# A later transpose of the softmax sums, and a short token chunk moved from last to third, in a fused attention and MLP kernel

## The chip, the cores and the metric

The kernel runs on one core of a Trainium2 chip. The metric is the device time of one execution in microseconds. Three runs of the kernel before took 754.11, 754.46 and 759.69 us; the median is 754.46 us. The profile comes from another execution, which took 759.01 us.

## The reference

Four batches, eight heads, 576 tokens, head size 64. Attention has a position bias that is itself a small network; its output, with the heads side by side, is a matrix of 2304 tokens by 512, which goes through a two-layer MLP with a squared ReLU.

```python
scores = np.matmul(q, k.transpose(0, 1, 3, 2)) / np.sqrt(D)
x = (np.log1p(np.abs(rel)) / psi_i)[..., None]
bias = np.maximum(x @ w1 + b1, 0.0) @ w2            # 8 heads, 576 x 576
scores = scores + bias.transpose(2, 0, 1)[None]
attn = np.exp(scores - np.max(scores, axis=-1, keepdims=True))
attn = attn / (np.sum(attn, axis=-1, keepdims=True) + 1e-09)
x = np.matmul(attn, v)   # then tokens x 512
h = x @ w_in             # 512 -> 2048
g = s * np.maximum(h, 0.0) ** 2 + b
return g @ w_out         # 2048 -> 512
```

All of it is float32. The kernel gets that from TensorE by splitting an operand into a high and a low part and adding three products (high by high, high by low, low by high).

## The kernel before, in words

There are three stages. In the first, to about 60 us, the bias of all heads is computed and written to DRAM. In the second, attention runs over 16 *pairs*: a pair p is one head of two batches. In the third, the MLP runs over chunks of tokens. The order of instructions on every engine is the program's own, written out by hand; each engine works through its queue in order and waits on semaphores.

A pair has five blocks of rows, numbered t or u from 0 to 4. Blocks 0 to 3 are 128 rows of each of the two batches; block 4 holds the last 64 rows of both in one tile of 128. The attention loop has 80 steps; `step(n)` with n = 5p + u works on three pairs' stages at once:

- the scores of block m = n + 2 (`scores`, line 228): TensorE writes them to PSUM, one tile for each of the two batches (`width`), out of a pool of two tiles;
- `biased` (line 242), on VectorE, adds the bias and takes the row maximum, once for each of these tiles, which it thereby gives back;
- `expo` (line 253), on ScalarE, exponentiates and adds up each row into a column of the pair's tile `su`;
- `probs_t` transposes the exponentials of block n on TensorE, through two PSUM tiles of the pool `ps_t`: part 2 (line 307) is the 128 columns at the seam of the two batches, part 0 and part 1 four transposes each (line 298). In u = 4 there are only part 1 (line 318) and part 0 (line 313), in this order. ScalarE (lines 303, 308, 320) and VectorE (305, 315) copy them to SBUF;
- `av` multiplies the transposed exponentials of the pair before, p - 1, with V (lines 333 and 336). Its last call, in u = 4, scales the result with the reciprocals of the sums (line 341, VectorE) and stores it (line 342, SP's queue);
- `fill` does the next piece of a background job, the decoding of the MLP's weights from their raw words: ScalarE (line 373), GpSimd (375), and three VectorE instructions (377, 380, 383), in a cycle of five; the weights of the first group are also split into parts (392, 395). A step does one or two such pieces, two where u is even. The raw words are loaded (line 360) two tiles ahead.

GpSimd also splits q and k of the next pair (lines 203 and 204), in u = 0 and u = 1.

The sums reach line 341 in this way. In u = 3 all sums of the pair are there, and `norm` (lines 265 and 266, VectorE) takes their reciprocals. `norm_t` transposes the 128 x 9 tile on TensorE into a free part of the PSUM tile of part 2 (line 270), and VectorE copies it out (line 272). `norm_store` writes it to DRAM with four small DMAs (278, 280), `norm_load` (285) reads it back as two broadcast rows in the layout of line 341. These DMAs stand in SP's queue with all other loads and stores.

In the third stage a chunk of n tokens takes 16 steps f. `expand` (line 430) makes 128 hidden features of all n tokens in 12 matmuls, ScalarE and VectorE apply the squared ReLU (434, 435, 439, 440), and `project` (line 454), two steps behind, adds their part to n/128 output tiles in PSUM with three matmuls each. At f = 15 each output tile is copied out (462, 464) and stored (465). The tokens of the next chunk are loaded (411) at f = 10 to 13 and split (419, 420) at f = 12 to 15. 2304 tokens make four chunks of 512 and one of 256, which is the last.

Of the kernel before, what the change touches and what calls it, by code (L numbers as in the profile page):

```python
# [26 lines left out]
def attention_moe(ctx, tc, q, k, v, w_in, w_out, dist, par, out):  # L27
# [3 lines left out]
    NT = out.shape[0]  # L31
# [10 lines left out]
    LAST = 5 * NP  # L42
# [144 lines left out]
    def load_q(p):  # L187
        if p < NP:
            h, b0 = pairs[p]
            qs[p] = io.tile([128, 640], F32, tag="qt", name="qt")  # L190
            nc.sync.dma_start(out=qs[p], in_=q[b0 // 2, h])

    def load_k(p):
        if p < NP:
            h, b0 = pairs[p]
            ks[p] = io.tile([128, S + 64], F32, tag="kt", name="kt")
            nc.sync.dma_start(out=ks[p], in_=k[b0 // 2, h])
# [16 lines left out]
    def scores(n):  # L214
        p, t = divmod(n, 5)
        qt, kt = qs[p], ks[p]
        c = slice(128 * t, 128 * t + 128)
        xs = range(width(n))
        ps = [ps_s.tile([128, 2, 512], F32, tag="s", name="sps") for _ in xs]
        mms = []  # L220
        for hf in range(2):
            for x in xs:
                d = slice(64 * x, 64 * x + 64) if t < 4 else slice(0, 128)
                o = hf * HALF + (64 if x == 0 else 0)
                for i, (a, b) in enumerate(((0, 0), (0, 1), (1, 0))):
                    mms.append((i, hf, x, ps[x][:, hf, 0:HALF], qt[d, a, c], kt[d, b, o:o + HALF]))
        for i, _, _, o, a, b in sorted(mms, key=lambda e: e[1::-1]):
            nc.tensor.matmul(o, a, b, start=(i == 0), stop=(i == 2))  # L228
        units[n] = (
            tp.tile([128, 2, S], F32, tag="pr", name="pr"),  # L230
            sm.tile([128, 2], F32, tag="mn", name="mn"),
            ps,
        )
        if t == 0:
            sums[p] = sm.tile([128, 9], F32, tag="su", name="su")

    def biased(n, x):
        p, t = divmod(n, 5)
        _, mn, ps = units[n]
        bias = bts[group[p]][:, t, 64 - 64 * x:64 - 64 * x + S] if t < 4 else bes[p]  # L240
        tt = tp.tile([128, S], F32, tag="tt", name="tt")
        nc.vector.tensor_tensor_reduce(  # L242
            tt.rearrange("p (a b) -> p a b", a=2), ps[x][:, :, 0:HALF],
            bias.rearrange("p (a b) -> p a b", a=2),
            -1.0 / ROOT, BIG, ALU.add, ALU.min, mn[:, x:x + 1],
        )
        tts[n, x] = tt

    def expo(n, x):
        p, t = divmod(n, 5)  # L250
        pr, mn, _ = units[n]
        col = 4 * x + t if t < 4 else 8
        nc.scalar.activation(  # L253
            pr[:, x], tts.pop((n, x)), AF.Exp, bias=mn[:, x:x + 1], scale=-1.0,
            accum_out=sums[p][:, col:col + 1])

    def width(n):
        return 2 if n % 5 < 4 else 1
# [4 lines left out]
    def norm(p):  # L263
        su = sums.pop(p)
        nc.vector.tensor_scalar(su, su, 1e-9, None, op0=ALU.add)
        nc.vector.reciprocal(su, su)
        rows[p] = su

    def norm_t(p, ps):
        nc.tensor.transpose(ps[0:9, 128:256], rows.pop(p), ident)  # L270
        rt = sm.tile([9, 128], F32, tag="rt", name="rt", bufs=2)
        nc.vector.tensor_copy(rt, ps[0:9, 128:256])
        rts[p] = rt

    def norm_store(p):
        rt = rts.pop(p)
        for x in range(2):
            nc.sync.dma_start(
                out=rs_d[p][x, 0:512].rearrange("(t j) -> t j", j=128), in_=rt[4 * x:4 * x + 4, :])
            nc.sync.dma_start(out=rs_d[p][x:x + 1, 512:S], in_=rt[8:9, 64 * x:64 * x + 64])  # L280

    def norm_load(p):
        rbs[p] = tp.tile([128, S], F32, tag="rb", name="rb", bufs=2)
        for x in range(2):
            nc.sync.dma_start(out=rbs[p][64 * x:64 * x + 64, :], in_=rs_d[p][x:x + 1, :].broadcast_to([D, S]))

    def probs_t(n, part):
        p, t = divmod(n, 5)
        pr = units[n][0]
        if p not in pts:  # L290
            pts[p] = (ptp.tile([128, 4, 2, S], F32, tag="pt", name="pt"),
                      ptp.tile([128, S], F32, tag="ptr", name="ptr"))
        pt, ptr = pts[p]
        ps = ps_t.tile([128, 512], F32, tag="t", name="tps")
        c = slice(128 * t, 128 * t + 128)
        if t < 4 and part < 2:
            for kb in range(4):
                nc.tensor.transpose(  # L298
                    ps[:, 128 * kb:128 * kb + 128],
                    pr[:, part, 64 * part + 128 * kb:64 * part + 128 * kb + 128], ident)  # L300
            o, i = pt[:, :, part, c], ps.rearrange("p (a b) -> p a b", a=4)
            if part == 0:
                nc.scalar.activation(o, i, AF.Copy)  # L303
            else:
                nc.vector.tensor_copy(o, i)  # L305
        elif t < 4:
            nc.tensor.transpose(ps[:, 0:128], pr.rearrange("p x j -> p (x j)")[:, 512:640], ident)  # L307
            nc.scalar.activation(ptr[:, c], ps[:, 0:128], AF.Copy)  # L308
            if t == 3:
                norm_t(p, ps)  # L310
        elif part == 0:
            for kb in range(4):
                nc.tensor.transpose(  # L313
                    ps[:, 128 * kb:128 * kb + 128], pr[:, 0, 128 * kb:128 * kb + 128], ident)
            nc.vector.tensor_copy(
                pt[:, :, :, 512:S], ps.rearrange("p (a x b) -> p a x b", a=4, x=2))
        else:
            nc.tensor.transpose(ps[0:64, 0:128], pr[:, 0, 512:S], ident)  # L318
            for x in range(2):
                nc.scalar.activation(  # L320
                    ptr[64 * x:64 * x + 64, 512:S], ps[0:64, 64 * x:64 * x + 64], AF.Copy)

    def av(p, kb, hf):
        h, b0 = pairs[p]
        pt, ptr = pts[p]
        vt = vals[p]
        if kb == 0 and hf == 0:
            accs[p] = ps_x.tile([128, 2, 512], F32, tag="x", name="xps")
        ps = accs[p]
        c = slice(hf * HALF, (hf + 1) * HALF)  # L330
        if kb < 4:
            for x in range(2):
                nc.tensor.matmul(ps[64 * x:64 * x + 64, hf, 0:HALF], vt[:, 4 * x + kb, :], pt[:, kb, x, c],  # L333
                                 start=(kb == 0), stop=False)
        else:
            nc.tensor.matmul(ps[:, hf, 0:HALF], vt[:, 8:10].rearrange("p i d -> p (i d)"), ptr[:, c],  # L336
                             start=False, stop=True)
        if kb == 4 and hf == 1:
            xs = rbs.pop(p)
            xv = xs.rearrange("p (a b) -> p a b", a=2)  # L340
            nc.vector.tensor_tensor(xv, ps[:, :, 0:HALF], xv, op=ALU.mult)
            nc.sync.dma_start(out=xt_d[b0 // 2][:, h * D:(h + 1) * D, :], in_=xs)
# [52 lines left out]
        nc.gpsimd.tensor_tensor(lo, full, hi.bitcast(F32), op=ALU.subtract)  # L395


    chunks = [(t0, min(512, NT - t0)) for t0 in range(0, NT, 512)]
    NC = len(chunks)
    xs_t, gs_t, os_t = {}, {}, {}  # L400

# [66 lines left out]
    def ok(n, x):  # L468
        return 0 <= n < LAST and x < width(n)
# [7 lines left out]
    def step(n):  # L477
        p, u = divmod(n, 5)
        m = n + 2
        cur = 0 <= n < LAST  # L480
        if ok(m, 0):
            scores(m)
            biased(m, 0)
        if cur and u == 3:
            norm(p)
        if ok(m, 1):
            biased(m, 1)
        if cur:
            for part in (2, 0, 1) if u < 4 else (1, 0):
                probs_t(n, part)  # L490
        if ok(m, 0):
            expo(m, 0)
        if ok(m, 1):
            expo(m, 1)
        if p >= 1:
            av(p - 1, u, 0)
            av(p - 1, u, 1)
            fill()
            if u % 2 == 0:
                fill()  # L500
        if 0 <= n < LAST:
            if u == 3:
                load_be(p + 1)
                load_q(p + 3)
                load_k(p + 3)
                norm_store(p)
            if u == 4:
                norm_load(p)
            if u < 2:
                split_qk(p + 1, u)  # L510
            if u == 4:
                load_v(p + 2)
            for e in loads_at.get((p, u), ()):
                load_bias(*e)
# [14 lines left out]
    def fill():  # L529
        next(filler, None)  # L530
# [189 lines left out]
```

## Time and profile before

| | |
|---|---|
| median of three runs | 754.46 us |
| the profiled execution | 759.01 us, its span 757.0 us |
| TensorE busy (matmuls) | 722.6 us, 95% of the span |
| VectorE busy | 428.3 us, 57% |
| ScalarE busy | 362.5 us, 48% |
| GpSimd busy | 185.4 us, 24% |
| mean granted TensorE clock | 0.991 |
| longest entries of the chain that ended last | line 430 26%, line 454 26%, line 228 8%, line 333 7%, line 298 7% |

Busy shares are means over the whole span, in which the three stages have different limits. Matmuls are pipelined and the ends of their bars are modelled, so starts are surer than ends. PE is TensorE's matmuls, PEld its weight loads, DVE VectorE, ACT ScalarE, POOL GpSimd and SP the engine from whose queue the DMAs are issued (SPq).

### The profile page before, as it was taken

How to read it: one execution, taken by the hardware profiler on the slowest of the kernel's cores; microseconds unless marked ns; L12 is line 12 of the kernel's file. 1: busy time of each engine (PE TensorE's matmuls, PEld its weight loads, DVE VectorE, ACT ScalarE, POOL GpSimd, SP SyncE). 2: the span in 40 equal slices, each digit the busy share in tenths (PEclk: the TensorE clock that was granted, in tenths of full speed). 3: DMA queues.
4: the chain of work that ended last, by engine and by line, in shares of the span. 5: the costliest groups of instructions: out<-in, count | busy, mean ns of one | idle time of the engine just before them, and what ended most of it. 6: DMA issues, size and time to landing. Idle time of an engine off the chain costs nothing.

```text
span 757.0 us, 12033 instructions
## 1 busy us (share of the span) xinstructions
PE 722.6 (95%) x4530; PEld 538.3 (71%) x4530; DVE 428.3 (57%) x794; ACT 362.5 (48%) x756; POOL 185.4 (24%) x194
## 2 busy tenths in 40 slices
PE   8978989898999999999999999999999999999998
PEld 5436666565666666666888888888888888888896
DVE  7966867687787877894369742233323333232332
ACT  7967656465666666664454432223222232222332
POOL 7990524344141252310755200000000000000000
PEclk9999999899999999999999999999999999999999
DMA  5878654545363664334012121000300002000100
GB/s 168 281 219 265 196 181 156 181 156 209 128 209 128 211 225 156 128 114 172 17 38 88 42 79 34 1 1 0 112 1 0 1 1 83 1 1 0 57 1 28
DMA packets 39817, 76.98 MB, mean 102 GB/s; under 512 B 9040, under 2 KB 12368, under 8 KB 39760
## 3 DMA queue, kind: packets, MB, share of 16 engines
q1 hardware_dynamic: 39616, 75.90, 30.7%
q8 instruction: 35, 0.57, 0.3%
q10 hardware_dynamic: 144, 0.33, 0.1%
q14 instruction: 22, 0.18, 0.1%
HBM read 55.45 MB, written 20.13 MB: 100 GB/s over the span
## 4 chain that ended last, share of the span: by engine, by line
PE 81%; POOL 6%; DVE 5%; issue 4%; DMA 2%; SPq 1%; ACT 1%; POOLq 0%; DVEq 0%
PE hps L430 26%; PE o L454 26%; PE sps L228 8%; PE xps L333 7%; PE tps L298 7%; POOL f L119 4%; DVE tt L242 3%; PE xps L336 2%; PE tps L307 1%; PE tps L313 1%; DMA raw<-in_moe_w_in_dram 1%; PE tps L318 0%; SPq L154 0%; DMA pt__110<-in_par_dram 0%; POOL kr L204 0%
## 5 line engine op out<-in xcount | busy, mean ns | idle before, releaser
L454 PE MATMUL o<-who,gt 128*128 128x512 f32 x576 | 192.4, 393 | 0.0
L430 PE MATMUL hps<-x,whi 128*128 128x512 f32 (+1 forms) x640 | 183.7, 371 | 0.0
L435 DVE SCALAR_TENSOR_TENSOR r<-r,sb 128x512 f32<-128x512 f32 (+1 forms) x80 | 56.7, 709 | 192.3 <-ACT r L434 192.3
L434 ACT ACTIVATE r<-hps 128x512 f32<-128x512 f32 (+1 forms) x80 | 44.5, 557 | 223.7 <-PE hps L430 223.7
L430 PEld LDWEIGHTS hps<-x,whi 128*128 128x128 f32 x640 | 116.9, 188 | 23.8 <-issue 0.4
L454 PEld LDWEIGHTS o<-who,gt 128*128 128x128 f32 x576 | 108.2, 188 | 24.2
L430 PE MATMUL hps<-x,wli 128*128 128x512 f32 (+1 forms) x320 | 118.7, 371 | 0.0
L253 ACT ACTIVATE pr<-tt,mn 128x576 f32<-128x576 f32 x144 | 110.2, 767 | 13.9 <-DVE mn L242 13.4
L242 DVE CUSTOM_DVE_ANT_0 tt<-sps,bt 128x576 f32<-128x576 f32 x128 | 92.3, 749 | 39.6 <-PE sps L228 34.8
L454 PE MATMUL o<-wlo,gt 128*128 128x512 f32 x288 | 113.2, 393 | 0.0
L228 PEld LDWEIGHTS sps<-kr,qr 64*128 64x128 f32 (+1 forms) x864 | 69.5, 187 | 42.1 <-DVE mn L242 16.9
L228 PE MATMUL sps<-kr,qr 64*128 64x288 f32 (+1 forms) x864 | 90.9, 313 | 6.5 <-POOL kr L204 2.9
L440 DVE SCALAR_TENSOR_TENSOR gt<-r,sb,gt 128x512 fp32r<-128x512 f32 (+1 forms) x80 | 56.3, 704 | 54.0 <-ACT gt L439 54.0
L298 PE MATMUL tps<-ident,pr 128*128 128x128 f32 x512 | 79.6, 285 | 0.9 <-ACT ptr L308 0.3
L439 ACT ACTIVATE gt<-r,sb 128x512 fp32r<-128x512 f32 (+1 forms) x80 | 54.4, 680 | 52.3 <-DVE r L435 52.3
L333 PE MATMUL xps<-pt,vt 128*64 128x288 f32 x512 | 78.4, 430 | 0.0
L298 PEld LDWEIGHTS tps<-ident,pr 128*128 128x128 f32 x512 | 58.5, 144 | 13.4 <-ACT ptr L308 9.0
L430 PEld LDWEIGHTS hps<-x,wli 128*128 128x128 f32 x320 | 60.1, 188 | 11.0
L454 PEld LDWEIGHTS o<-wlo,gt 128*128 128x128 f32 x288 | 54.1, 188 | 11.6
L305 DVE COPY pt<-tps 128x512 f32<-128x512 f32 x64 | 44.0, 688 | 17.4 <-PE tps L298 17.4
L303 ACT ACTIVATE pt<-tps 128x512 f32<-128x512 f32 x64 | 38.3, 598 | 32.0 <-PE tps L298 30.3
L375 POOL TENSOR_SCALAR full<-full 128x512 f32<-128x512 f32 x32 | 21.0, 657 | 127.0 <-ACT full L373 120.6
(69 smaller groups left out, 742.1 us busy)
## 6 DMA issues: line engine op xcount, KB each, us to landing
bias<-stg SPq DMA_DIRECT2D x36, 288.0 KB
raw<-in_moe_w_in_dram SPq DMA_DIRECT2D x16, 512.0 KB
raw<-in_moe_w_out_dram SPq DMA_DIRECT2D x16, 512.0 KB
bt<-bias SPq DMA_DIRECT2D x7, 1152.0 KB
qt<-in_q_dram SPq DMA_DIRECT2D x16, 320.0 KB
kt<-in_k_dram SPq DMA_DIRECT2D x16, 320.0 KB
vt<-in_v_dram SPq DMA_DIRECT2D x16, 320.0 KB
rb<-rs SPq DMA_DIRECT2D x32, 144.0 KB
```

Of the source, the lines that this page charges most:

```text
L228: nc.tensor.matmul(o, a, b, start=(i == 0), stop=(i == 2))
L242: nc.vector.tensor_tensor_reduce(tt.rearrange("p (a b) -> p a b", a=2), ps[x][:, :, 0:HALF], bias.rearrange("p (a b) -> p a b", a=2), -1.0 ...
L253: nc.scalar.activation(pr[:, x], tts.pop((n, x)), AF.Exp, bias=mn[:, x:x + 1], scale=-1.0, accum_out=sums[p][:, col:col + 1])
L298: nc.tensor.transpose(ps[:, 128 * kb:128 * kb + 128], pr[:, part, 64 * part + 128 * kb:64 * part + 128 * kb + 128], ident)
L305: nc.vector.tensor_copy(o, i)
L333: nc.tensor.matmul(ps[64 * x:64 * x + 64, hf, 0:HALF], vt[:, 4 * x + kb, :], pt[:, kb, x, c], start=(kb == 0), stop=False)
L430: nc.tensor.matmul(ps[:, 0:n], w[0, g][:, a, fc], xs_t[c, a][:, j, 0:n], start=(i == 0), stop=(i == 3 * KB - 1))
L434: nc.scalar.activation(r, ps[:, 0:n], AF.Relu)
L435: nc.vector.scalar_tensor_tensor(r, r, sb[:, 0:1], r, op0=ALU.mult, op1=ALU.mult)
L439: nc.scalar.activation(hi, r, AF.Identity, bias=sb[:, 1:2])
L440: nc.vector.scalar_tensor_tensor(lo, r, sb[:, 1:2], hi.bitcast(F32), op0=ALU.add, op1=ALU.subtract)
L454: nc.tensor.matmul(os_t[c][i], gt[:, a, tok], w[1, g][:, fo], start=(f == 0 and j == 0), stop=(f == NF - 1 and j == 2))
```

## The change

There are two parts. In the first, `norm_t` is called one step later, in u = 4 behind part 1 of `probs_t`, and in that PSUM tile; in u = 3, `norm` comes behind both calls of `biased` and no longer between them. The stores of the sums move from u = 3 to u = 4, and the loads from u = 4 to u = 0 of the next pair (for the last pair, to the step n = LAST). In the second part, the chunk of 256 tokens is put third: tokens 1024 to 1280; the chunks behind it start at 1280 and 1792.

```diff
@@ probs_t
         elif t < 4:
             nc.tensor.transpose(ps[:, 0:128], pr.rearrange("p x j -> p (x j)")[:, 512:640], ident)
             nc.scalar.activation(ptr[:, c], ps[:, 0:128], AF.Copy)
-            if t == 3:
-                norm_t(p, ps)
         elif part == 0:
...
             for x in range(2):
                 nc.scalar.activation(
                     ptr[64 * x:64 * x + 64, 512:S], ps[0:64, 64 * x:64 * x + 64], AF.Copy)
+            norm_t(p, ps)
@@ chunks
-    chunks = [(t0, min(512, NT - t0)) for t0 in range(0, NT, 512)]
+    sizes = [512] * (NT // 512)
+    if NT % 512:
+        sizes.insert(len(sizes) // 2, NT % 512)
+    chunks = [(sum(sizes[:i]), n) for i, n in enumerate(sizes)]
@@ step
             biased(m, 0)
+        if ok(m, 1):
+            biased(m, 1)
         if cur and u == 3:
             norm(p)
-        if ok(m, 1):
-            biased(m, 1)
...
+        if n == LAST:
+            norm_load(p - 1)
         if 0 <= n < LAST:
             if u == 3:
                 load_be(p + 1)
                 load_q(p + 3)
                 load_k(p + 3)
+            if u == 4:
                 norm_store(p)
-            if u == 4:
-                norm_load(p)
+            if u == 0 and p > 0:
+                norm_load(p - 1)
```

## Rows read from the trace of the kernel before

**Rows 1.** Busy time by stage: us, each engine's busy us (instructions), PEclk, DMA share, GB/s

```profile
60.00:345.00 285.00, 262.01 (x2028) 177.04 (x2026) 221.02 (x500) 184.01 (x464) 91.74 (x88) 0.98 0.53 175
362.00:702.00 340.00, 340.00 (x1477) 276.99 (x1476) 132.80 (x169) 106.56 (x174) 36.91 (x30) 1.00 0.09 28
702.00:757.00 55.00, 51.28 (x314) 45.43 (x312) 18.43 (x37) 16.11 (x36) 0.00 (x0) 1.00 0.08 29
```

**Rows 2.** Waits, 60 to 345 us: who waited for whom; us in total, times, longest

```profile
PE tps L270 <- DVE su L266: 16.9, 15, 1.2
PEld tps L298 <- DVE rt L272: 3.8, 14, 0.3
PE sps L228 <- POOL kr L204: 2.9, 4, 1.3
```

**Rows 3.** Timeline: start, us, instruction; the scores issued in u=3, u=4, u=0, u=1

```profile
236.18 1.06 PE L228 MATMUL sps<-kr,qr 64*128 64x288 f32 x12
...
241.10 1.07 PE L228 MATMUL sps<-kr,qr 64*128 64x288 f32 x12
...
243.73 1.07 PE L228 MATMUL sps<-kr,qr 64*128 64x288 f32 x12
...
247.17 1.06 PE L228 MATMUL sps<-kr,qr 64*128 64x288 f32 x12
```

**Rows 4.** Timeline inside that u=3; in brackets the idle time before

```profile
237.17 0.33 PE L307 MATMUL tps<-ident,pr 128*128 128x128 f32 x1
...
238.05 0.17 DVE L265 TENSOR_SCALAR su<-su 128x9 f32<-128x9 f32 x1
...
238.62 0.27 PE L270 MATMUL tps<-ident,su 128*9 128x128 f32 x1 [1.12 <-DVE su L266]
...
238.72 1.32 PE L298 MATMUL tps<-ident,pr 128*128 128x128 f32 x8
...
239.06 0.27 DVE L272 COPY rt<-tps 9x128 f32<-9x128 f32 x1
...
239.38 0.42 PEld L298 LDWEIGHTS tps<-ident,pr 128*128 128x128 f32 x4 [0.30 <-DVE rt L272]
...
240.08 0.69 DVE L305 COPY pt<-tps 128x512 f32<-128x512 f32 x1 [0.75 <-PE tps L298]
```

**Rows 5.** Busy time by stretch, one where the clock fell (columns as in rows 1)

```profile
105.50:108.90 3.40, 3.35 (x15) 2.47 (x17) 1.97 (x5) 2.09 (x5) 0.00 (x0) 0.50 0.17 60
```

**Rows 6.** Timeline of VectorE at the end of u=4 and the start of u=0

```profile
243.56 0.69 DVE L315 COPY pt<-tps 128x512 f32<-128x512 f32 x1
...
244.16 0.75 DVE L341 TENSOR_TENSOR rb<-xps,rb 128x576 f32<-128x576 f32 x1
...
244.94 0.76 DVE L242 CUSTOM_DVE_ANT_0 tt<-sps,bt 128x576 f32<-128x576 f32 x1
```

**Rows 7.** Timeline: a decode beside GpSimd's split, and the same decode alone

```profile
179.47 1.54 POOL L204 TENSOR_TENSOR kr<-kt,kr 128x640 fp32r<-128x640 f32 x1
...
179.65 1.91 DVE L380 SCALAR_TENSOR_TENSOR full<-raw,full 128x512 uint32<-128x512 uint32 x1
...
227.40 0.69 DVE L380 SCALAR_TENSOR_TENSOR full<-raw,full 128x512 uint32<-128x512 uint32 x1
```

**Rows 8.** Timeline at the end of attention: stores, load and use of the last sums

```profile
346.56 0.21 SPq L280 DMA_DIRECT2D rs<-rt  x1
...
352.05 1.11 SPq L285 DMA_DIRECT2D rb<-rs  x2
...
360.11 0.74 DVE L341 TENSOR_TENSOR rb<-xps,rb 128x576 f32<-128x576 f32 x1
```

**Rows 9.** Chain that ended last, in the short chunk: start, us, what

```profile
702.37 1.42 PE hps L430 x12
...
715.05 1.41 PE o L454 x6
```

**Rows 10.** Timeline of SP's queue: the four output stores of a long chunk

```profile
625.43 2.22 SPq L465 DMA_DIRECT2D out_dram<-ob  x4
```

## The prediction

> **What bounds the kernel now.** I read the busy time by stage first [rows 1]. From 362 to 702 us TensorE (PE) is busy 340.00 of 340.00 us: five chunks of tokens run there with no gap, over three chunk borders too. So an edit in that stage can win nothing unless it takes matmuls away. The attention stage, 60 to 345 us, is different: PE is busy 262 of 285 us, so 23 us are lost there, while VectorE (DVE) has 64 us of idle time and ScalarE (ACT) 101. No engine is full; the order of waits sets the time.
>
> The second view is the list of waits in that stage [rows 2]. One entry holds most of PE's idle time: 16.9 us in 15 waits, at the transpose of the sums (line 270), for the reciprocal on DVE (line 266). A sibling stands beside it: 3.8 us in 14 waits in which the next transposes wait for the copy of that transpose (line 272), since it holds one of the two PSUM buffers. Waits for GpSimd's split of k are a sixth of the first, 2.9 us.
>
> The third view is the timeline of one pair, read by the start of each step's scores [rows 3]. Step u=3 takes 4.92 us (236.18 to 241.10), u=4 2.63, and u=0 3.44. Step u=3 has the same matmuls as u=0 plus one small transpose, yet lasts 1.48 us longer. Inside it [rows 4] the reason is plain: PE ends the transpose of the small block at 237.5, then DVE must finish the first reduction and both small operations of the norm, the first of which starts at 238.05, and PE starts again at 238.62, 1.12 us idle. Everything after it in the step, the copies and the products with V, is shifted by this.
>
> **The change, part by part.** The profiled execution took 759.01 us, its span 757.0; the three runs have a median of 754.46. The sum is made on the profiled execution and taken off the median.
>
> 1. *The two waits go.* In the new order the norm is computed in u=3 behind both reductions, and its transpose is asked for in u=4, one whole step (some 3.4 us) after. PE then has nothing to wait for: the reciprocal, only some 0.7 us later than now, is ready well before u=4 starts. That removes 16.9 + 3.8 = 20.7 us of waits [rows 2]. The one pair checks it: 1.12 + 0.30 [rows 4] of the 1.48 us by which its u=3 is too long [rows 3]. What is late next in u=3: the scores of u=4 need both PSUM tiles of scores back, which is the end of the second reduction. That reduction moves forward to 238.05, where the norm's first instruction stands now, and lasts 0.76 as the one of rows 6, so it ends near 238.8, while PE, by the pace of u=0, wants it at 236.18 + 3.44 = 239.6. It holds by 0.8 us.
>
> 2. *Clock.* Three of the long u=3 steps are followed by stretches at half the granted clock (1.2 in place of 2.4 GHz), as 105.5 to 108.9 [rows 5]; there are three such stretches, one of them twice as long, and around each PE had stalled twice, for GpSimd's k and for the norm. One of the two stalls goes. What half the clock costs is at most half of 4 x 3.4 us, 6.8, and less by the time in which PE waits; the least is 0. I take 2, since the stall for k stays [rows 2].
>
> 3. *The transpose itself moves to u=4.* It is one of the small transposes, of which eight take 1.32 us [rows 4], or 0.15 to 0.17 each, in a step where PE has no gap (2.63 us). 16 times 0.15 is 2.4 us lost; in u=3 it is given back within the wait already counted.
>
> 4. *The copy of it, 0.27 us* [rows 4], moves on DVE into u=4. There it stands before the copy of probabilities, the scaling of the output and then the first reduction of the next pair, which follow each other at 243.56, 244.16 and 244.94 with no gap [rows 6]. Its cover is that in u=0 PE needs 3.44 us [rows 3] where the loop scores, two reductions, scores needs only 2.63, so a late DVE has 0.8 us to spare. With two decode operations on DVE in that step (0.69 each [rows 7]) the cover is gone and the full 0.27 comes through. Bounds: 0 and 15 x 0.27 = 4.1. Two of five positions of the decode sequence put two such operations there, 6 of 15 pairs: 1.6 us.
>
> 5. *DVE's slack in u=3 goes.* Before, DVE idles in that step while the chain waits, 0.75 us ahead of the copy alone [rows 4]. Afterwards it has two reductions (0.76 each), the norm (0.17 and about as much again), the copy (0.69) and a decode (0.69): 3.2 us of a step of 3.4. The nearest row for a bad case is a decode that ran beside GpSimd's split of k: 1.91 us in place of 0.69 [rows 7]. Such an excess, 1.22 us, is now hidden in part by u=3's slack. Bounds 0 and 15 x 1.22 = 18.3; DVE is idle for 64 us of the stage [rows 1], the copies still have slack in u=1 and u=2, so I take a value near the low end, 1.5 us.
>
> 6. *The DMAs.* The four stores of the sums go to u=4, behind the store of the output on SP's queue, and the two loads to u=0 of the next pair; they are needed in u=4 of that pair, over 10 us on. That hides them. The loads wait for the stores to land, with SP's later loads behind them: raw weights, bias rows, q and k. Those are asked for two tiles or two pairs ahead, so a few us don't show. At the end of attention it is tighter: the last stores went out at 346.56, the load at 352.05, and the scaling ran at 360.11 [rows 8]. Moved, the stores leave a little before the place of the present load, say at 351, and by the same 5.5 us the load leaves at 356.5, with 3.6 us left to land: I take 0, at worst 3 us. GpSimd's queue is passed by no moved instruction that it issues.
>
> 7. *The short chunk third.* The same matmuls in another order: a step of it takes 1.42 for the first product and 1.41 for the second [rows 9], and stays at that. The next chunk's tokens are now loaded inside it, two steps (5.7 us) before they are split; the pieces per chunk are 1, 2, 2, 2, 1 in both orders. At the end four tiles are stored in place of two, but four such stores were issued in 2.22 us elsewhere [rows 10], at the pace at which PE finishes them, so the last lands no later. Taken at 0, bounds -1 and +2.
>
> Sum: 20.7 + 2 - 2.4 - 1.6 - 1.5 = 17.2 us off. On the profiled execution 741.8, on the median 754.5 - 17.2 = **737**. The favourable ends (20.7 + 5, nothing lost) give 754.5 - 25.7 = 729; the costs of parts 3 to 5 (5.5) at two and a half times their value give 745.
>
> **A rule against it.** The row first: at 179.65 a decode with two operands in SBUF lasted 1.91 us, and its neighbour on GpSimd ran from 179.47 to 181.01 [rows 7]. The Trainium skill, "SBUF — State Buffer", section "Who interferes with whom", says that such a VectorE instruction is locked out for the whole of a GpSimd instruction that reads SBUF; the trace agrees (1.91 against 0.69). That page's lock is a mechanism of the second rival below.
>
> **The rivals.**
> - *The gain arrives* (forecast): 729 to 743, chance 0.62.
> - *DVE becomes the bound of u=3 to u=0.* Each collision like that at 179.65 costs 1.22 us, and with the slack of u=3 gone it reaches the next reduction, so the next scores. For it: no gap before the reduction at 244.94 [rows 6]. Against it: DVE's 64 idle us. In half the pairs it takes 7 x 1.22 = 8.5 more: 746; in all of them, 15 x 1.22 = 18.3 more, which is 755 and no change. Chance 0.20, a quarter of it for the latter.
> - *More is won:* the clock stays up and DVE hides its additions, 722 to 729. Chance 0.07.
> - *Another wait takes the whole place,* for raw weights or k that a faster attention asks for sooner: 750 to 757. Against it: the wait for k is 2.9 us now [rows 2]. Chance 0.06.
> - *Slower.* SP's queue. The load of the sums, at its head in u=0, stands until the stores have landed, 5.5 us by rows 8, and the raw weights behind it land after ACT has reached their first decode step; ACT stops with the exponentials behind it. It decides from the point at which SP's delay exceeds the lead of a raw tile, which is ten decode steps, at eight to a pair more than a pair's length; for a slower kernel PE would have to lose over 17.2 / 15 = 1.15 us in each pair, and at 1.8 the time is 754.5 - 17.2 + 27 = 764. For it: SP held by landings now too. Against it: that lead. Chance 0.05.
>
> **How the numbers follow.** A difference under 1%, 7.5 us, can't be told from none. Faster than 746.9: the forecast, the larger gain, and three quarters of the DVE case, 0.62 + 0.07 + 0.15 = 0.84. Same: 0.05 + 0.06 = 0.11. Slower 0.05. The range 728 to 747 holds the forecast, the mild DVE case and half of the larger gain, and leaves out about 0.2.
>
> **What would show it.** Right: no wait of PE at the transpose of the sums and none of the next transposes for its copy; u=3 at 3.4 to 3.6 us, u=4 at 2.7 to 2.9; attention's PE idle time under 8 us; the chunks at the same 340 us without a gap. Wrong: u=3 still above 4.2 with PE waiting for the second reduction, or u=0 and u=1 grown by what u=3 lost (then DVE bounds); scores waiting longer for k; a gap in PE after the short chunk or before the first product of the second stage at 362.

## The result: 1.3% faster, where 2.3% was forecast

In four runs each the changed kernel took 747.5 us (median; 745.43 to 749.34) and the kernel before 756.91 (754.11 to 759.69): a ratio of 0.987, with an interval of 0.983 to 0.991. The forecast was 737, or 17.2 us off; 9.4 us came. The range ended at 747, so the measured median stands half a microsecond over its end; as ratios to the 754.46 us that it was worked out from, the range is 0.965 to 0.990, and the measured 0.987 lies in it, near the slow end. The profiled execution of after took 748.03 us, its span 746.2 against 757.0.

### The profile after

First the busy time by stage, in the columns of [rows 1]. Attention now ends near 336 us and no longer at 345; the second line is the hand-over to the MLP's second product, the third 338 us of the chunks.

```profile
60.00:336.00 276.00, 258.02 (x2060) 175.84 (x2059) 227.11 (x510) 189.94 (x475) 92.91 (x88) 0.99 0.60 188
336.00:352.00 16.00, 15.84 (x79) 10.69 (x78) 4.85 (x8) 5.49 (x10) 4.77 (x4) 0.97 0.20 73
352.00:690.00 338.00, 338.00 (x1560) 279.54 (x1559) 136.49 (x185) 108.82 (x189) 35.81 (x29) 1.00 0.09 30
```

PE has no gap in the chunks, before and after. In attention it now lacks 18.0 of 276 us, 23 of 285 before [rows 1]. The forecast wanted under 8.

The list of waits, 60 to 340 us, says who PE waits for now, its two longest entries. The columns are those of [rows 2].

```profile
PE tps L270 <- ACT ptr L318: 13.6, 16, 5.6
PE sps L228 <- POOL kr L204: 2.7, 4, 1.3
```

The two entries that the forecast wanted gone, 16.9 and 3.8 us [rows 2], are gone. At the same line 270 another one stands: the transpose of the sums waits for ScalarE's copies (line 318 of after), 16 times, 13.6 us. One of them lasts 5.6 us; the other 15 make 8.0, 0.53 each. The timeline of a pair's u=4 and of the steps at its two ends shows where (here and in the timelines below, rows in between are left out):

```profile
223.78 1.07 PE L228 MATMUL sps<-kr,qr 64*128 64x288 f32 x12
226.34 0.17 DVE L265 TENSOR_SCALAR su<-su 128x9 f32<-128x9 f32 x1
227.18 1.06 PE L228 MATMUL sps<-kr,qr 64*128 64x288 f32 x12
228.17 0.30 PE L316 MATMUL tps<-ident,pr 128*64 128x128 f32 x1
228.50 0.45 ACT L318 ACTIVATE ptr<-tps 64x64 f32<-64x64 f32 x2 [0.82 <-PE tps L316]
229.00 0.28 PE L270 MATMUL tps<-ident,su 128*9 128x128 f32 x1 [0.53 <-ACT ptr L318]
229.12 0.60 PE L311 MATMUL tps<-ident,pr 128*128 128x128 f32 x4
...
230.62 1.06 PE L228 MATMUL sps<-kr,qr 64*128 64x288 f32 x12
```

Step u=3 takes 227.18 - 223.78 = 3.40 us (4.92 before), and u=4 takes 230.62 - 227.18 = 3.44 (2.63 before, [rows 3]). The norm's first instruction runs at 226.34, 2.6 us before the transpose, so its input is not what is late. The small transpose of part 1 ends near 228.5, ScalarE copies its two halves out, and only then may PE write the sums into a free part of the same PSUM tile. All else of the step stands behind that in PE's queue.

Summed over the 14 inner pairs, from scores to scores: u=3 went from 77.3 to 51.3 us (26.0 less), u=0 to u=2 from 145.2 to 141.4 (3.7 less), u=4 from 37.4 to 48.2 (10.8 more). The last scores of attention start 17.6 us sooner, at 322.53 and not at 340.15. From the first product of the MLP's second stage to the end both kernels take 395.0 us. What is left is between: 21.8 us from the last scores to that product before, 28.7 after. So 6.9 of the 17.6 us are given back there; 17.6 - 6.9 = 10.7, the difference of the spans but for 0.1. The timeline of that stretch, in order of time over all engines:

```profile
318.32 0.26 SPq L280 DMA_DIRECT2D rs<-rt  x1
322.53 1.07 PE L228 MATMUL sps<-kr,qr 128*128 128x288 f32 x6
325.41 1.11 SPq L285 DMA_DIRECT2D rb<-rs  x2
326.62 1.96 SPq L414 DMA_DIRECT2D x<-xt  x4
328.18 0.30 PE L316 MATMUL tps<-ident,pr 128*64 128x128 f32 x1
330.58 1.94 ACT L422 ACTIVATE x<-x 128x512 fp32r<-128x512 f32 x3 [3.40 <-DMA x<-xt]
333.58 0.43 ACT L318 ACTIVATE ptr<-tps 64x64 f32<-64x64 f32 x2
334.06 0.38 PE L270 MATMUL tps<-ident,su 128*9 128x128 f32 x1 [5.58 <-ACT ptr L318]
346.75 1.11 SPq L285 DMA_DIRECT2D rb<-rs  x2
350.27 0.76 DVE L340 TENSOR_TENSOR rb<-xps,rb 128x576 f32<-128x576 f32 x1 [1.17 <-DMA rb<-rs]
351.18 0.47 PE L457 MATMUL o<-who,gt 128*128 128x512 f32 x1 [0.16 <-DVE rb L340]
```

Read it from the end of the chain back. PE stands 5.58 us at line 270 for the copies of line 318; these stand in ScalarE's queue behind the splits of the first chunk's tokens (422); the splits wait 3.40 us for their tokens; the tokens' loads (414) stand in SP's queue behind the load of the pair's sums (285), which waits from 318.6 to 325.4 for the sums' stores to land. Then, from 333.4 to 336.8 us, the granted clock is 0.5, a stretch that is not there before; and at the end the scaling (340) waits 1.17 us for the last sums' rows, and PE 0.16 for it. SP's own list of waits has it for the whole stage. Before, 60 to 345 us:

```profile
SPq L285 <- DMA rs<-rt: 6.8, 4, 5.1
```

After, 60 to 340 us:

```profile
SPq L285 <- DMA rs<-rt: 90.3, 16, 7.6
```

### The profile page after: what moved, and what is told of

It is laid out like the page before. It is cut to its first block, busy times and chain, and to the rows that moved or that the text cites. A ratio compares the mean times of both kernels' runs of the same rounds, so it can differ in the third digit from the quotient of the medians.

```text
span 746.2 us, 12023 instructions
## 1 busy us (share of the span) xinstructions
PE 717.1 (96%) x4530; PEld 534.2 (72%) x4530; DVE 429.9 (58%) x794; ACT 363.8 (49%) x756; POOL 186.6 (25%) x194
## 4 chain that ended last, share of the span: by engine, by line
PE 76%; DMA 5%; issue 3%; POOL 3%; ACT 1%; DVE 1%; SPq 1%; DVEq 0%; POOLq 0%; ACTq 0%
PE o L457 27%; PE hps L433 26%; PE sps L228 8%; PE tps L298 6%; PE xps L332 6%; DMA rs<-rt 3%; PE xps L335 2%; PE tps L307 1%; POOL kr L204 1%; PE tps L311 1%; ACT ptr L318 1%; DMA raw<-in_moe_w_in_dram 1%; POOL qr L204 1%; DMA x<-xt 1%; PE tps L270 0%
## 5 line engine op out<-in xcount | busy, mean ns | idle before, releaser
L228 PE MATMUL sps<-kr,qr 64*128 64x288 f32 (+1 forms) x864 | 88.8, 314 | 4.7 <-POOL kr L204 2.7
L298 PE MATMUL tps<-ident,pr 128*128 128x128 f32 x512 | 76.3, 280 | 0.3 <-ACT ptr L308 0.3
L332 PE MATMUL xps<-pt,vt 128*64 128x288 f32 x512 | 75.8, 418 | 0.0
L298 PEld LDWEIGHTS tps<-ident,pr 128*128 128x128 f32 x512 | 56.8, 141 | 11.6 <-ACT ptr L308 11.4
L374 POOL TENSOR_SCALAR full<-full 128x512 f32<-128x512 f32 x32 | 22.6, 706 | 116.2 <-ACT full L372 115.7
L136 PE MATMUL bps<-f,pt__110 128*32 128x512 f32 x288 | 44.6, 624 | 5.3 <-POOL f L119 2.2
L332 PEld LDWEIGHTS xps<-pt,vt 128*64 128x64 f32 x512 | 31.2, 136 | 23.9 <-issue 10.0
```

Source lines behind the costliest of these rows:

```text
L136: nc.tensor.matmul(pb[32 * c:32 * c + 32, 0:512], w2bd, fs[c][0][:, 0:8], start=True, stop=True)
L298: nc.tensor.transpose(ps[:, 128 * kb:128 * kb + 128], pr[:, part, 64 * part + 128 * kb:64 * part + 128 * kb + 128], ident)
```

## The experiments

The theory: the missing size is (a) the wait for ScalarE's copies in u=4 and (b) the hand-over, where SP's queue, ScalarE's queue and that same wait act one behind the other. The rivals: VectorE, now without slack, makes the long steps; the order of the chunks takes its part; the stretches at half clock do. Times are medians; the ratio is to the kernel before measured beside each kernel, whose median there was 758.8 to 760.7 us.

### The transpose of the sums asked for first

```diff
     def norm_t(p, ps):
-        nc.tensor.transpose(ps[0:9, 128:256], rows.pop(p), ident)
...
         else:
+            nc.tensor.transpose(ps[0:9, 128:256], rows.pop(p), ident)
             nc.tensor.transpose(ps[0:64, 0:128], pr[:, 0, 512:S], ident)
```

> The changed kernel with one thing moved: in u=4 the transpose of the sums is asked for ahead of the transpose of the last block, so both write the PSUM tile before anyone reads it. Theory A (u=4 grew from 2.63 to 3.44 us because PE waits at the transpose of the sums for ScalarE's two copies out of the same PSUM tile): u=4 falls to 2.7 to 2.9 us, 15 x 0.6 = 9 us less in the loop, and the 5.6 us wait of PE at the end of attention goes, of which 2 to 4 us come through; 734 to 738 against 747.5. Theory B (u=4 grew because VectorE's extra copy of 0.27 us and its order delay the reductions): u=4 stays at 3.2 us or more, 744 or more.

740.03 us, ratio 0.975 (0.972 to 0.978). The timeline of u=4 has no wait of PE left, with the sums' transpose ahead of part 1's:

```profile
222.14 1.06 PE L228 MATMUL sps<-kr,qr 64*128 64x288 f32 x12
223.14 0.28 PE L315 MATMUL tps<-ident,su 128*9 128x128 f32 x1
223.25 0.27 PE L316 MATMUL tps<-ident,pr 128*64 128x128 f32 x1
223.36 0.60 PE L310 MATMUL tps<-ident,pr 128*128 128x128 f32 x4
224.86 1.06 PE L228 MATMUL sps<-kr,qr 64*128 64x288 f32 x12
```

u=4 takes 2.72 us, 0.09 over the 2.63 before: this is what the transpose itself costs, and 0.72 was the wait. Over the inner pairs u=4 falls from 48.2 to 38.1. But u=0 and u=1 grow from 95.7 to 100.8 together, with single steps up to 4.2 us, in which the next scores wait for VectorE's reductions (line 242): half of what was won comes back as VectorE's lateness, which the wait in u=4 had covered. That, and a hand-over of still 26.8 us with a stretch at half the granted clock in it (325.7 to 329.1), puts the time 2 us over what was expected. The mechanism (a) is shown; its worth is 7.5 us, not 10.

### The chunk order alone, and the later norm alone

Added to before, and then taken out of after:

```diff
-    chunks = [(t0, min(512, NT - t0)) for t0 in range(0, NT, 512)]
+    sizes = [512] * (NT // 512)
+    if NT % 512:
+        sizes.insert(len(sizes) // 2, NT % 512)
+    chunks = [(sum(sizes[:i]), n) for i, n in enumerate(sizes)]
```

> The kernel before with the short chunk third and nothing else. Theory A (the order of chunks is worth nothing, since PE has no gap in that stage): ratio 1.000, within 0.3%; PE without a gap through all chunks. Theory B (the order costs or gives part of what was missing, by a late load or by the last stores): 2 us or more either way, seen as a gap after the short chunk or as a longer end.

759.25 us, ratio 1.001 (0.999 to 1.004). The busy time of the chunks, in the columns of [rows 1], is full again:

```profile
362.00:702.00 340.00, 340.00 (x1569) 281.07 (x1568) 137.06 (x186) 110.26 (x190) 37.33 (x30) 1.00 0.09 29
```

> The changed kernel with the chunks in their old order, so the part on the sums alone. Theory A: the whole of the change's effect, some 9 to 11 us less than before (0.986), u=3 at 3.40 and u=4 at 3.44. Theory B (the chunk order took part of the gain): over 13 us less than before.

747.78 us, ratio 0.985 (0.982 to 0.989), with u=3 at 3.39 and u=4 at 3.44. All of the gain and all of the missing size lie in the moved norm; the chunk order is worth nothing.

### Only the order of the reductions

Before, with the transpose left in u=3 but the norm behind both reductions, so that the wait grows and nothing else is moved:

```diff
-        if cur and u == 3:
-            norm(p)
         if ok(m, 1):
             biased(m, 1)
+        if cur and u == 3:
+            norm(p)
```

> The kernel before with only the order on VectorE changed: both reductions ahead of the norm, while the transpose of the sums stays in u=3. Theory A (PE's wait for the reciprocal is what made u=3 long): the reciprocal comes one reduction later, 0.68 us, so u=3 goes from 4.92 to about 5.6 and the time up by 16 x 0.68 = 11 us, 768. Theory B (something else sets the length of u=3 and the wait is only where it shows): u=3 stays within 0.2 us and the time within 3 us.

783.46 us, ratio 1.032 (1.029 to 1.036): slower, as expected, by twice the size. PE's wait at the transpose, then one place of it and what follows, then one stretch of the busy time (columns as in rows 1):

```profile
PE tps L270 <- DVE su L266: 28.8, 15, 2.6
```

```profile
253.14 0.27 PE L270 MATMUL tps<-ident,su 128*9 128x128 f32 x1 [1.79 <-DVE su L266]
254.37 2.17 PE L333 MATMUL xps<-pt,vt 128*64 128x288 f32 x8
```

```profile
254.40:257.80 3.40, 3.40 (x19) 2.06 (x20) 1.29 (x2) 1.59 (x5) 0.00 (x0) 0.50 0.03 9
```

The waits grew by 28.8 - 16.9 = 11.9 us, the size expected. The other half is the clock: 13 stretches, twelve of 3.4 us and one of twice that, run at half the granted clock in attention, mostly 20.5 us apart as the stalls are, against three before, and the eight products of line 333 take 2.17 us in it, where they took 1.19 in a step of before at full clock. The pairs separate the two halves: in the two inner pairs without such a stretch (5 and 10) u=3 takes 5.46 and 5.49 us, near the 5.6 expected, and in the twelve with one 6.45 to 8.79, the longest of them with a wait for k too. This is part 2 of the prediction seen in reverse, and the order of the reductions pays only together with the later transpose.

### The hand-over, piece by piece

First the last scores' step ahead of the token splits in ScalarE's queue, the rest as in after:

```diff
-    for work in (att, xsp, xsp, xsp, xsp, att, h0, att, h0, att,
+    for work in (att, att, xsp, xsp, xsp, xsp, h0, att, h0, att,
```

> The changed kernel with one word moved at the end of attention: step 79 stands ahead of the four splits of the first chunk's tokens, no longer behind them. Theory A (PE's 5.6 us wait there is a chain: the transpose of the sums waits for ScalarE's copies, these stand behind the splits, the splits wait for the token loads): the wait falls to the 0.5 us of every other pair, the loop stays as it is (u=4 at 3.44), and from the last scores to the first product of the second stage it takes 24 us in place of 28.7; 743. Theory B (the time is set by the token loads alone, in whatever order the splits stand): within 1.5 us of 747.5.

745.93 us, ratio 0.985 (0.980 to 0.989). Timeline of the hand-over:

```profile
327.96 0.28 PE L270 MATMUL tps<-ident,su 128*9 128x128 f32 x1 [0.54 <-ACT ptr L318]
333.16 0.63 ACT L422 ACTIVATE x<-x 128x512 fp32r<-128x512 f32 x1 [1.86 <-DMA x<-xt]
346.67 0.76 DVE L340 TENSOR_TENSOR rb<-xps,rb 128x576 f32<-128x576 f32 x1 [2.15 <-DMA rb<-rs]
```

The 5.58 us at line 270 are 0.54, so they came from the splits ahead of the copies. The hand-over falls only from 28.7 to 26.1 us, since the tokens still come late and the sums' rows now end the wait in their place. In time, 1.6 us against after is too little to decide.

Next the sums' load behind the tokens' loads in program order (u=2 in place of u=0), nothing else:

```diff
-            if u == 0 and p > 0:
+            if u == 2 and p > 0:
                 norm_load(p - 1)
```

> The changed kernel with the load of the sums two steps later (u=2 in place of u=0), so that at the end of attention the loads of the first chunk's tokens stand ahead of it in SP's queue. Theory A (that load, waiting some 7 us for its stores to land, held the token loads back): ScalarE no longer waits 3.4 us for tokens, the first part of the end of attention is 3 to 4 us shorter; 743 to 745; SP's wait for the stores falls under 30 us in all from 90. Theory B (the token loads wait for their buffers, not for SP): unchanged, 747.5.

741.7 us, ratio 0.980 (0.975 to 0.986). Timeline of the splits and the transpose, then SP's wait at its head:

```profile
325.34 2.18 ACT L422 ACTIVATE x<-x 128x512 fp32r<-128x512 f32 x4
327.90 0.28 PE L270 MATMUL tps<-ident,su 128*9 128x128 f32 x1 [1.16 <-ACT ptr L318]
```

```profile
SPq L285 <- DMA rs<-rt: 86.7, 15, 7.3
```

The splits wait for no token, and the hand-over falls to 23.8 us: the tokens behind the sums' load were 4.9 of the 6.9 us that it had grown by, the stretch at half clock included, which is not there in this profile. The expectation that SP's wait would fall under 30 us is wrong. SP runs ahead of the steps and stands at the load whatever step it is written in; what the edit changes is what is queued behind it.

Then the three edits together, and with them the copy of the transposed sums on ScalarE:

> The three edits together: the transpose of the sums first in its tile, step 79 ahead of the splits, the load of the sums in u=2. Theory A: the loop as with the first edit alone (last scores at 316 us), and from there 22 to 23 us to the first product of the second stage, as in the kernel before (21.8) in place of 26.8; 735 to 737. Theory B (VectorE, without gaps at the end of attention, takes the place): 739 or more, as with the first edit alone.

736.87 us, ratio 0.973 (0.968 to 0.977). The time is as expected, the hand-over is not: 24.9 us. Its timeline has the lateness in a new place, since the earlier scaling (340) waits for its rows and DVE's share of the splits (423) stands behind it:

```profile
322.43 0.76 DVE L340 TENSOR_TENSOR rb<-xps,rb 128x576 f32<-128x576 f32 x1 [0.83 <-DMA rb<-rs]
323.84 0.50 PE L433 MATMUL hps<-x,whi 128*128 128x512 f32 x1 [1.95 <-DVE x L423]
```

```diff
-        nc.vector.tensor_copy(rt, ps[0:9, 128:256])
+        nc.scalar.activation(rt, ps[0:9, 128:256], AF.Copy)
```

> The three edits together and the copy of the transposed sums on ScalarE in place of VectorE. Theory A (with the waits gone, VectorE bounds u=0 and u=1 in pairs with two decodes behind u=4, so that the 0.27 us copy comes through there): u=0 and u=1 lose about half of what they have over 3.40, 2 to 3 us in all, against the three edits alone. Theory B (the copy is hidden): within 1 us of the three edits alone.

737.11 us, ratio 0.974 (0.969 to 0.978). u=0 and u=1 fall from 99.4 to 98.2 us: 1.2 us where 2 to 3 were expected, near the 1.6 us that part 4 gave for this copy, and the time does not follow.

Last of this group, the transpose first and the load late, without the reordered splits:

> Two of the three edits: the transpose of the sums first in its tile and the load of the sums in u=2; step 79 behind the splits as in the changed kernel. Theory A (in the three edits together VectorE, which stood at the scaling of the pair before until its sums had been read back, held up the splits by 2 us): the end of attention, from the last scores to the first product of the second stage, falls from 24.9 to 22.5 to 23.5 us; 735. Theory B (it is bound by the sums of the last pair coming back, whatever stands before): 24.5 or more.

737.3 us, ratio 0.969 (0.966 to 0.971). The hand-over takes 24.7 us, as in theory B, and the third edit shows no gain beside the other two. What still ends the wait is in the timeline: the sums' stores go out, their load leaves 8.2 us after, and the scaling and PE wait for it.

```profile
327.51 0.27 SPq L279 DMA_DIRECT2D rs<-rt  x1
335.99 1.12 SPq L284 DMA_DIRECT2D rb<-rs  x2
339.84 0.76 DVE L340 TENSOR_TENSOR rb<-xps,rb 128x576 f32<-128x576 f32 x1 [4.35 <-DMA rb<-rs]
340.75 0.47 PE L457 MATMUL o<-who,gt 128*128 128x512 f32 x1 [3.34 <-DVE rb L340]
```

Behind this stall of 3.34 us comes a stretch at half clock (341.6 to 345.0), and the time from that product to the end is 396.6 us, 1.5 more than in the kernel that follows.

### The sums' stores ahead of the output's store

The same kernel, with the four small stores put ahead of the pair's 288 KB output store in SP's queue:

```diff
+        if cur and u == 4:
+            norm_store(p)
         if p >= 1:
             av(p - 1, u, 0)
...
-            if u == 4:
-                norm_store(p)
```

> The same with the four stores of the sums ahead of the store of the output in SP's queue. Theory A (the last thing that the second stage waits for is the way of the last pair's sums through DRAM, some 7 us from the last store to the load): the stores leave 2 us sooner and the wait before the first product goes; 1 us less than with the two edits. Theory B (the first product is bound by its own stage): no difference over 0.5 us.

732.66 us (732.21 to 733.57), ratio 0.963 (0.962 to 0.965): the fastest of all, and 4.6 us under the one before it, where 1 was expected. The timeline of the last pair, the busy time of attention and of the hand-over, and SP's waits at the first store and at the load:

```profile
322.90 0.33 SPq L279 DMA_DIRECT2D rs<-rt  x1
328.16 1.10 SPq L284 DMA_DIRECT2D rb<-rs  x2
334.41 0.76 DVE L340 TENSOR_TENSOR rb<-xps,rb 128x576 f32<-128x576 f32 x1 [0.86 <-DMA rb<-rs]
335.31 0.47 PE L457 MATMUL o<-who,gt 128*128 128x512 f32 x1
```

```profile
60.00:314.00 254.00, 248.95 (x1999) 170.51 (x1995) 216.96 (x492) 181.42 (x455) 92.39 (x88) 1.00 0.60 194
314.00:335.00 21.00, 21.00 (x123) 14.45 (x122) 10.94 (x21) 10.79 (x24) 3.33 (x3) 1.00 0.51 167
```

```profile
SPq L277 <- DVE rt L271: 66.7, 16, 6.2
SPq L284 <- DMA rs<-rt: 4.3, 4, 2.7
```

PE has no gap in the hand-over, which takes 21.3 us, and lacks 5.0 of 254 us in attention, with the granted clock at 1.00. SP's wait at the load falls from some 90 us to 4.3. SP does not stand idle less for that: it now waits 66.7 us at the first of the four stores, for VectorE's copy of the sums (line 271). But the way of the sums is shorter. Counted from the last scores, the last store of the last pair leaves 2.6 us sooner than in the kernel above, and the load goes 4.9 us behind it where it went 8.2; of these 5.9 us the hand-over takes 3.5. In part the stores are sooner; in part they land sooner; in part the issues of the output store and of the next loads, some 1.6 us, now stand between them and the load and cover their landing. The clock has a share too: of the 6.9 us between the two profiled executions 1.5 lie behind the hand-over and 1.4 in u=3 of pair 4, where the kernel above has stretches at half clock and this one has none.

One more try was made at VectorE's lateness, the copy of part 0 in u=4 on ScalarE:

```diff
-            nc.vector.tensor_copy(
-                pt[:, :, :, 512:S], ps.rearrange("p (a x b) -> p a x b", a=4, x=2))
+            nc.scalar.activation(
+                pt[:, :, :, 512:S], ps.rearrange("p (a x b) -> p a x b", a=4, x=2), AF.Copy)
```

> The same again, with the 0.69 us copy of part 0 in u=4 on ScalarE in place of VectorE. Theory A (VectorE bounds u=0 and u=1 once the waits are gone): the sum of these two steps over pairs 1 to 14 falls from 99.4 to 96 or less, 95.2 being two times 14 x 3.40, and the time by 3 us. Theory B (ScalarE becomes the bound of u=4, which has two copies and two exponentials there): u=4 grows from 2.72 to 3.2 or more and the time rises.

734.05 us, ratio 0.964 (0.961 to 0.967). u=1 falls from 51.3 to 48.8 us and u=0 grows from 48.2 to 50.1, to 3.77 us in several pairs; u=4 stays at 2.72, so neither theory came. In u=0 PE now waits for a copy of ScalarE (60 to 310 us; there was one such wait, of 0.3 us, before this edit):

```profile
PE tps L297 <- ACT ptr L307: 1.8, 6, 0.3
```

What VectorE gains, ScalarE loses one step sooner. u=0 and u=1 are bound by the two together; nothing is won.

## Why the prediction was right, and where its size failed

- *Part 1, the two waits* (20.7 us): right in u=3: they are gone, and the second reduction is not late in u=3, which takes 3.40 us as forecast in ten of the 14 inner pairs; the other four wait for k, and the mean is 3.66. Its "PE then has nothing to wait for" is what did not hold in u=4 (part 3).
- *Part 2, the clock* (2 us): the mechanism is right, shown in reverse by the order of the reductions alone, and the term was too small. The three stretches around the norm are gone from the middle of attention. By an estimate they cost 4.6 us: their pairs took 7.29, 8.10 and 7.27 us in u=3, which is 1.4, 1.7 and 1.5 more than 4.92 and what their wait for k still adds in after (4.38, 4.92 and 4.22 against 3.40). The stall for k that stays is enough in some executions: in four later profiles (the three edits, with and without the copy on ScalarE, two of the three, and the copy of part 0 on ScalarE) a stretch follows it in pair 4, from 135.8 to 138.3 us on, and u=3 takes 6.3 to 6.4 us there. One stretch came at 333.4, in the hand-over. Another, 53.5 to 60.3 us, is not there in the profile of before; it comes and goes between profiles whose program is the same up to there, and with it the scores of the sixth block started 2.9 us later (69.6 and 66.7 us).
- *Part 3, the transpose in u=4*: **the step that failed.** It was priced at its own duration, 0.15 us, "in a step where PE has no gap", which gave 2.4 us. The step grew by 0.81 us: 0.09 for the transpose (u=4 is 2.72 with it asked for first) and 0.72 for a wait (0.53 of it as PE's idle time in the timeline). The row for it was in the trace of before, in ScalarE's timeline of that u=3:

```profile
237.53 0.28 ACT L308 ACTIVATE ptr<-tps 128x128 f32<-128x128 f32 x1 [1.60 <-PE tps L307]
```

  There the transpose followed a copy of ScalarE out of its PSUM tile too, but the copy ended at 237.8 and the reciprocal only by 238.6 [rows 4], so PE's entry in the list of waits had the later of the two alone. The weight load of the same transpose had the other, in the same list, 60 to 345 us, and the prediction did not price it:

```profile
PEld tps L270 <- ACT ptr L308: 20.0, 16, 1.3
```

  In u=4 the reciprocal is early, and the copy is what is left. The Trainium skill, "Perfetto Trace Analysis", section "Matmuls", says that independent matmul groups should rotate through PSUM banks so that the evacuation of one lies beside the next; the trace agrees (0.53 us of wait in one tile), and here the other order in the same tile did it without another bank.
- *Parts 4 and 5, VectorE* (3.1 us): right as a mechanism, but hidden in after: u=0 to u=2 even fell by 3.7 us, because the wait in u=4 gave DVE time. With that wait gone it appears, 5.1 us in u=0 and u=1, of which the copy of part 4 is 1.2. The second rival is therefore real and small.
- *Part 6, the DMAs* (0, at worst 3 us): mis-sized, 6.9 us. The landing of the last sums was watched, as it should, but not what stands behind their load in SP's queue; that is 4.9 us of it, by the later load. The landing was also taken at the 5.5 us of before, where the sums' stores stood a step ahead of the output's store and the load's delay was mostly SP's wait for VectorE's scaling (6.8 us of waits for landing in all); the change put them behind that store, and in the last pair the load went 7.1 us after the last of them. It was the mechanism of the slower rival, at one place, with the tokens in the part of the raw weights; no wait of PE in attention's list goes back to the raw weights.
- *Part 7, the chunks* (0): right, 1.001 (0.999 to 1.004).

By the sum, on the profiled executions: 17.2 forecast; less 8.4 in part 3 (10.8 against 2.4), 6.9 in part 6 and 2.9 for the stretch at 53.5; more 3.1 of DVE's cost that did not come, 3.7 that u=0 to u=2 gave, and 3.3 in u=3 (26.0 against 22.7 of parts 1 and 2). That makes 9.1 of the 10.8 us between the spans; the rest is u=3 and u=4 of the first pair, which together went from 6.7 to 5.2 us. That the time came into the range is thus in part luck: 18.2 us were lost that the sum did not have, and 10.1 us won that it did not have either. The forecast's own case, 729 to 743, did not come, and what took the rest was not the rival of VectorE that the range was widened for. Not shown is why the stretch at 53.5 us comes in some executions, nor which share of the 4.6 us of the last improvement is the earlier stores, which their sooner landing and the cover, and which the clock.

## What to carry to other kernels

An instruction that is moved away from a wait takes its other waits along, and PE's entry in the list of waits shows only the one that ended last: read the weight load's entry beside it, look for every engine that reads or writes the same PSUM tile, and put the writer whose input is ready first. On a DMA queue a load that waits for a store to land holds all that is behind it, so its place among the others, not its step, is what counts; small stores that are soon read back go ahead of a large one. And where a wait is taken out of a loop, look at its end too: the last turn meets other work.

## What the runs showed of the hardware

- Four small stores into DRAM, issued right behind the output's store (128 x 576 float32, 288 KB) in the same queue, let a load that depends on them go 7.1 us (after) and 7.3 us (transpose first, load late) behind the last of them, the median of 16 pairs each. Issued ahead of it they let it go 2.4 us behind the last of them, as the median, and 1.1 to 2.1 us behind the large store's own issue in 13 of the 16 pairs. In the last pair of that kernel, where the four stores stand behind four loads of 512 KB, it was still 4.9 us. The Trainium skill, "DMA: Bandwidth & Descriptors", section "Queues, rings and completion order", says that a DMA's semaphore increment lands only after every earlier write of the same DMA engine; the order of the two medians agrees, though no run here shows the single engines.
- Stalls of PE of up to 2.6 us were followed by 13 stretches at half the granted clock in attention (the order of the reductions alone), where stalls of up to 1.3 were followed by three (before); the clock doubled the price of the waits (24 us for 11.9). The same stall does not always have it: PE's wait of 1.3 us for k in pair 4 was followed by such a stretch in four of the later profiles, and by none in after and in the fastest kernel.
